# Turning the short row blocks of an attention with all 128 rows, and shifting one head's keys in the copies out of PSUM

## The chip, the core and the metric

The kernel runs on one core of one Trainium2 chip. A core has five engines with a queue each: TensorE (PE; its weight loads are listed apart as PEld), VectorE (DVE), ScalarE (ACT), GpSimd (POOL) and SyncE (SP), which here issues nearly all transfers between HBM and SBUF. TensorE writes to PSUM; the other engines read from there. The metric is the device time of one execution in microseconds (us), as a median of several runs.

## The reference

Three layers follow each other, for a batch of 4, all in float32:

```python
def _attn_ref(q, k, v):                  # 4 x 8 heads x 576 rows x 64
    ...                                  # q and k are rotated by position
    scores = scale * np.matmul(q_rot, k_rot.transpose(0, 1, 3, 2))
    scores = scores - np.max(scores, axis=-1, keepdims=True)
    attn = np.exp(scores)
    attn = attn / (np.sum(attn, axis=-1, keepdims=True) + 1e-09)
    return np.matmul(attn, v)

def _moe_ref(x, mu_k, mu_r, w_k, w_v, w_r):   # x: 4 x 576 x 512
    ...                                  # xk, xr: mixes of a row and the row before
    k = np.maximum(xk @ w_k, 0.0)
    v = k * k @ w_v
    return 1.0 / (1.0 + np.exp(-(xr @ w_r))) * v

def _moe2_ref(x, w_in, w_spatial, b_spatial, w_out):
    h = np.maximum(x @ w_in, 0.0)
    ...                                  # u, v: halves of h; v is normalized, mixed over rows
    return (u * v_s) @ w_out
```

## The kernel before

**Units.** The attention works on pairs of heads: 16 pairs, four in a batch entry, with the two heads of a pair on partitions 0 to 63 and 64 to 127. The 576 rows of a pair are four blocks of 128 rows and a rest of 64. A *unit* is one block of 128 rows for both heads of a pair. The rests of two neighbouring pairs make one unit together, the *tail*: its tile of exponentials has, for each pair u, the 64 rows of the first head on partitions 0 to 63 and those of the second on 64 to 127. `which` gives nine units for two pairs, the fifth of them the tail; there are 72 units and eight tails.

**A unit's steps.** `scores` (TensorE, into the two-buffered PSUM tile `s`), `top` (VectorE: the two maxima, line 342), `expo` (ScalarE: the two exponentials with their sums into `pf`, called p or P, line 347), `total`, `norm` and `spread` (sum, reciprocal, and the reciprocals laid out as `rb`, lines 351, 354, 358), three `turn` steps (TensorE) and three `take` steps (two on ScalarE, one on VectorE), and for each two units one `values` (TensorE, line 402) and `gather` (VectorE, line 414). `turn` transposes P, since the multiplication with V needs the keys on the partitions: it multiplies a block of P, as the loaded weights, with an identity matrix, and the result stands in a PSUM tile `t`, of which there are two in turn. `take` copies it to the SBUF tile `pt`.

**The layout of `pt`.** Ten chunks of up to 320 columns. Chunks 0 to 3 hold the first head's keys 0 to 511, chunks 4 to 7 the second head's keys 64 to 575, chunk 8 the first head's keys from 512 (partitions 0 to 63) and the second head's keys 0 to 63 (partitions 64 to 127), and chunk 9 the reciprocals. So the second head's chunks begin 64 keys on. Columns 256 to 319 belong to the tail.

**A tail's turns before.** `turn(0)` and `turn(1)` (line 367) take one head n each, for both pairs: eight transposes of 64 rows by 128 keys, beginning at key 64 n. Both need both exponentials (line 431). `turn(2)` (line 373) puts the last or first 64 keys and the reciprocals into place by eight multiplications of 64 x 64, which are 16 instructions on the chip. `take` copies once for each pair: 128 x 256 for n = 0, 1 (ScalarE), 128 x 128 for n = 2 (VectorE), line 395. For other units the turns are lines 378, 380 and 381.

**What sets the order.** All steps of the attention and of the second layer's feed-forward part are given to `Plan` (`add`, `order`, from line 57 on) with an engine, an assumed cost, the steps that must be done before, and a rank. `order` simulates the five engines with these costs and always starts next, on the engine that is free first, the step with the lowest rank among those that could start soon; the sequence that comes out is the program's order on each engine. So another cost or another dependency of one step can move other steps too. A batch entry's feed-forward multiplications (`mk`, line 498, and `mv`, line 537, on TensorE) have ranks that spread them over the units of the next batch entry. The first batch entry's 18 units have none beside them.

Functions that the change touches, and what calls them:

## Time and profile before

| | |
|---|---|
| median of 3 runs | 777.41 us (776.02 to 779.28) |
| the profiled execution's own time | 777.82 us |
| its span, first to last instruction | 776.0 us |
| busy: TensorE, VectorE, ScalarE | 740.8, 481.0, 463.6 us |
| transposes of a tail (line 367) start at | 33.3, 78.2, 129.4, 189.1, 246.3, 303.8, 361.2, 416.8 us |
| last transposes of all (line 378) | 444 us |
| feed-forward multiplications begin | 108.9 us |

The span is what the trace covers; the rest of the execution's own time lies around it. Busy times of one engine can't be added to those of another, since the engines run beside each other. What follows 446 us is the gate and the third layer, in which TensorE multiplies with little pause. In rows of the timeline a matmul's duration overlaps with that of the next one; what TensorE takes for a group is read from the starts of one group to the next.

### The profile page before, as it was taken

To read this page: it belongs to the slowest core of one execution; us is meant where nothing else is said; L and a number is where in the kernel's file an instruction comes from. 1 tells how busy PE (TensorE), PEld (TensorE's weight loads), DVE (VectorE), ACT (ScalarE), POOL (GpSimd) and SP (SyncE) were. 2 spreads that over 40 slices of the span, in tenths; PEclk is the share of its full clock that TensorE was granted. 3 is DMA by queue.
4 is the path that set the end of the run, shared out by engine and by line. 5 is a ranking of instruction groups with operands and counts; after the bars stand their busy time and mean duration, and the time that the engine had idled before them with its cause. 6 is when DMAs were issued, how large, how long until landed. Compare 5 with 4: busy or idle time off the path is not lost.

```text
span 776.0 us, 14283 instructions
## 1 busy us (share of the span) xinstructions
PE 740.8 (95%) x5696; PEld 649.9 (84%) x5696; DVE 481.0 (62%) x881; ACT 463.6 (60%) x1061; POOL 112.2 (14%) x132
## 2 busy tenths in 40 slices
PE   4788889999999999999999999999999999999997
PEld 2555569788888888888888898989989999998997
DVE  5988898888777877687856434246463342545111
ACT  3878898778777878778777644245333322533221
POOL 1432424011211211211111000002020000101000
PEclk9999999999999999999999999999999999999999
DMA  8363540542342442533232175072201212010101
GB/s 294 116 201 122 175 129 20 164 149 99 134 163 85 141 156 88 182 113 126 92 131 70 51 268 210 24 264 57 87 1 62 63 46 77 17 31 1 62 1 62
DMA packets 35268, 84.13 MB, mean 108 GB/s; under 512 B 4545, under 2 KB 10433, under 8 KB 35202
## 3 DMA queue, kind: packets, MB, share of 16 engines
q1 hardware_dynamic: 34658, 82.63, 31.6%
q8 instruction: 45, 0.74, 0.4%
q10 hardware_dynamic: 544, 0.59, 0.3%
q14 instruction: 21, 0.17, 0.1%
HBM read 60.65 MB, written 22.55 MB: 107 GB/s over the span
## 4 chain that ended last, share of the span: by engine, by line
PE 88%; DVE 4%; ACT 3%; DMA 3%; issue 0%; SPq 0%; ACTq 0%
PE mv L537 13%; PE mk L498 11%; PE v L402 11%; PE t L378 9%; PE sp L673 8%; PE r L673 7%; PE u L673 7%; PE hv L737 6%; PE o L673 6%; PE s L330 6%; PE s L338 3%; ACT pf L347 1%; DVE raw L249 1%; DMA wi<-wd 1%; PE s L327 1%; DVE sm L342 1%
## 5 line engine op out<-in xcount | busy, mean ns | idle before, releaser
L342 DVE TENSOR_REDUCE sm<-s 128x1 f32<-128x576 f32 x144 | 107.2, 751 | 36.9 <-PE s L330 30.5
L347 ACT ACTIVATE pf<-s,sm 128x576 f32<-128x576 f32 x144 | 107.0, 745 | 14.1 <-DVE sm L342 13.0
L537 PE MATMUL mv<-kh,wv 128*128 128x288 f32 x512 | 114.1, 305 | 1.2 <-ACT kh L512 1.2
L498 PE MATMUL mk<-x,wk 128*128 128x288 f32 x768 | 110.2, 298 | 0.4 <-ACT rl L505 0.4
L395 ACT COPY pt<-t 128x512 f32<-128x512 f32 (+1 forms) x160 | 84.8, 542 | 34.3 <-PE t L378 32.0
L498 PEld LDWEIGHTS mk<-x,wk 128*128 128x128 f32 x768 | 102.9, 188 | 0.7 <-ACT rl L505 0.6
L378 PE MATMUL t<-ident,pf 128*128 128x128 f32 x512 | 82.5, 284 | 14.0 <-ACT pf L347 14.0
L537 PEld LDWEIGHTS mv<-kh,wv 128*128 128x128 f32 x512 | 85.6, 191 | 5.4 <-issue 3.9
L378 PEld LDWEIGHTS t<-ident,pf 128*128 128x128 f32 x512 | 56.6, 141 | 39.9 <-issue 16.4
L402 PE MATMUL v<-pt,vt 128*64 128x256 f32 (+1 forms) x640 | 87.5, 411 | 0.0
L537 PE MATMUL mv<-kl,wv 128*128 128x288 f32 x256 | 76.5, 299 | 0.6 <-DVE kl L516 0.6
L402 PEld LDWEIGHTS v<-pt,vt 128*64 128x64 f32 x640 | 44.3, 136 | 31.7 <-issue 4.1
L673 PE MATMUL sp<-ws,vn 128*128 128x288 f32 x384 | 53.9, 295 | 0.0
L673 PE MATMUL r<-xr,wr 128*128 128x288 f32 x384 | 52.5, 296 | 1.2 <-ACT vs L543 1.2
L673 PE MATMUL o<-g,wo 128*128 128x288 f32 x384 | 52.9, 296 | 0.5 <-ACT os L796 0.5
L673 PEld LDWEIGHTS r<-xr,wr 128*128 128x128 f32 x384 | 51.7, 188 | 1.8 <-ACT vs L543 1.5
L673 PEld LDWEIGHTS sp<-ws,vn 128*128 128x128 f32 x384 | 52.4, 188 | 0.7
L673 PEld LDWEIGHTS o<-g,wo 128*128 128x128 f32 x384 | 51.7, 188 | 1.4 <-ACT os L796 1.2
L673 PE MATMUL u<-x,wi 128*128 128x288 f32 x384 | 52.0, 296 | 0.0
L673 PEld LDWEIGHTS u<-x,wi 128*128 128x128 f32 x384 | 51.6, 188 | 0.3
L537 PEld LDWEIGHTS mv<-kl,wv 128*128 128x128 f32 x256 | 48.9, 191 | 1.2 <-DVE kl L516 1.2
L249 DVE TENSOR_TENSOR raw<-raw,cst 128x1152 f32<-128x1152 f32 (+1 forms) x34 | 45.6, 1344 | 5.7 <-DMA raw<-kp 4.9
(347 smaller groups left out, 1200.3 us busy)
## 6 DMA issues: line engine op xcount, KB each, us to landing
raw<-kp SPq DMA_DIRECT2D x15, 576.0 KB, 3.8
raw<-qp SPq DMA_DIRECT2D x15, 576.0 KB, 4.3
vt<-vp SPq DMA_DIRECT2D x16, 320.0 KB, 3.8
xd<-xt SPq DMA_DIRECT2D x16, 288.5 KB, 3.2
vd<-vs SPq DMA_DIRECT2D x32, 144.0 KB, 1.8
v<-vd SPq DMA_DIRECT2D x16, 288.0 KB, 2.7
out<-os SPq DMA_DIRECT2D x15, 288.0 KB, 2.1
wi<-wd SPq DMA_DIRECT2D x8, 512.0 KB, 9.1
```

The source lines that it names most:

```text
L249: nc.vector.tensor_tensor(t["raw", k][:, :, z], t["raw", k][:, :, z], cst[:, :, z], op=ALU.mult)
L330: nc.tensor.matmul(ps[j][:, h, :HALF], t[a, 0][r, 128 * c:128 * c + 128], t[b, 1][r, x], **f)
L338: nc.tensor.matmul(o, q[r, 128 * c:min(128 * c + 128, S)], k[r, h * HALF:(h + 1) * HALF], start=True, stop=True)
L342: nc.vector.tensor_reduce(st["sm"][:, 0, j:j + 1], st["s"][j][:, :, :HALF], axis=AX.XY, op=ALU.max, negate=True)
L347: nc.scalar.activation(st["p"][:, j, :].rearrange("p (a b) -> p a b", a=2), st["s"][j][:, :, :HALF], AF.Exp, bias=st["sm"][:, 0, j:j + 1], ...
L378: nc.tensor.transpose(pt[:, c, :], p[:, n, k:k + 128], ident)
L395: nc.scalar.copy(o, x) if eng == "ACT" else nc.vector.tensor_copy(o, x)
L402: nc.tensor.matmul(pv[HEAD[j], z], v[:, 4 * j + c if c < 4 else 8 + j, :], pt[:, 4 * j + c if c < 4 else 8, z], start=c == 0, stop=c == 4)
L498: nc.tensor.matmul(ps[:, :HALF], wk[w][:, c, fc * 128:(fc + 1) * 128], a[:, c, :], start=k == 0, stop=k == 11)
L537: nc.tensor.matmul(xs["v", dc][:, :HALF], wv[w][:, fc, dc * 128:(dc + 1) * 128], a, start=k == 0, stop=k == 23)
L673: nc.tensor.matmul(ps[:, h, :HALF], w, a[:, h * HALF:(h + 1) * HALF], start=m == 0, stop=m == n - 1)
L737: nc.tensor.matmul(ps[:, :FS], x[a][:, d, c:c + 128], wi[w][:, d, FS:], start=k == 0, stop=k == 11)
```

## The change

A tail's `turn(0)` and `turn(1)` now take one pair each instead of one head: four transposes of all 128 rows (both heads' rests) by 128 keys, beginning at key 0 for both heads. Each needs only its own pair's exponentials. `turn(2)` transposes the 64 keys from 512 on, with all 128 rows, once for each pair, and turns the reciprocals with four multiplications of 64 x 64 as before. By source calls a tail has 14 turns in place of 24. Since the second head's chunks begin 64 keys on, the copies put its halves from one half of the partitions to the other: `take` has three copies for n = 0, 1 (128 x 256 and two of 64 x 256) and six for n = 2 (four of 64 x 64, two of 128 x 64). The layout of `pt` changes so that these halves lie in a row: chunk 8 becomes chunk 4, and the second head's chunks become 4 (upper half) to 8. The costs that the plan assumes for the tail's turns and copies change with it, and a `take` of n = 0, 1 now belongs to one pair's `pt` alone.

```diff
         def turn(n, slot):
...
-            if tail and n < 2:
+            if tail and n == 2:
                 for u in range(2):
-                    for c in range(4):
-                        k = 64 * n + 128 * c
-                        nc.tensor.transpose(pt.rearrange("p c (h q) -> p (c h) q", h=2)[:, 4 * u + c, :],
-                                            p[HEAD[n], u, k:k + 128], ident[HEAD[n], HEAD[n]])
-            elif tail:
+                    nc.tensor.transpose(pt[0:64, u, :], p[:, u, 512:], ident)
                 for u in range(2):
-                    for k in range(2):
-                        for j, r in enumerate(HEAD):
-                            nc.tensor.matmul(pt[r, u, HEAD[k]], st["r"][r, u, :] if k else p[r, u, 512 - 512 * j:576 - 512 * j],
-                                             ident[r, r], start=True, stop=True)
+                    for j, r in enumerate(HEAD):
+                        nc.tensor.matmul(pt[r, 2 + u, 0:64], st["r"][r, u, :], ident[r, r], start=True, stop=True)
             elif n < 2:
                 for c in range(4):
-                    k = 64 * n + 128 * c
+                    k = (0 if tail else 64 * n) + 128 * c
                     nc.tensor.transpose(pt[:, c, :], p[:, n, k:k + 128], ident)
...
         def take(n, eng):
...
+            if not tail:
+                o = into[0]["pt"][:, :, 128 * part:128 * part + 128]
+                copy(o[:, 5 * n:5 * n + 4, :] if n < 2 else o[:, 4:10:5, :], x if n < 2 else x[:, 0:2, :])
+            elif n < 2:
+                o = into[n]["pt"]
+                copy(o[:, 0:4, z], x[:, :, lower])
+                copy(o[upper, 4:8, z], x[lower, :, upper])
+                copy(o[lower, 5:9, z], x[upper, :, upper])
+            else:
+                for u, d in enumerate(into):
+                    copy(d["pt"][lower, 4, z], x[lower, u, lower])
+                    copy(d["pt"][upper, 8, z], x[lower, u, upper])
+                    copy(d["pt"][:, 9, z], x[:, 2 + u, 0:64])
...
-        ready = [[exps[m, 0], exps[m, 1]] if tail else [exps[m, 0]], [exps[m, 1]], [sp]]
+        ready = [exps[m, 0], exps[m, 1], sp]
...
-            turned[m, n] = add("PE", (0.5, 0.5, 0.8)[n] if tail else (0.44, 0.44, 0.22)[n], lambda slot, n=n: turn(n, slot),
-                               ready[n], m + 0.1 * n, take="t", kind="t")
+            turned[m, n] = add("PE", (0.44, 0.44, 0.75 if tail else 0.22)[n], lambda slot, n=n: turn(n, slot),
+                               [ready[n]], m + 0.1 * n, take="t", kind="t")
...
-            x = add(eng, ((0.68, 0.68, 0.55) if tail else (0.59, 0.59, 0.42))[n], lambda n=n, eng=eng: take(n, eng),
-                    [turned[m, n]] + [y for d in into for y in freed.get(d["n"] - PTB, [])], m - 0.2, give=turned[m, n])
+            to = into if n == 2 else into[n if tail else 0:][:1]
+            x = add(eng, (1.13, 1.13, 0.95)[n] if tail else (0.59, 0.59, 0.42)[n], lambda n=n, eng=eng: take(n, eng),
+                    [turned[m, n]] + [y for d in to for y in freed.get(d["n"] - PTB, [])], m - 0.2, give=turned[m, n])
```

The order moves with it. TensorE at the first tail, before: s_379 are scores of unit 5, t_1 and t_2 the tail's turns 1 and 2, t_0_421 the first turn of unit 5, v_426 the multiplication with V of the first pair's tail, s_453 and s_454 the scores of unit 6.

```order
L338 MATMUL s_379<-rot_1_259,rot_0_262 128x288
L367 MATMUL t_1_389<-ident,pf_357 128x64 x8
L373 MATMUL t_2_405<-ident,pf_357 64x64 x2
L373 MATMUL t_2_405<-ident,rb_401 64x64 x2
...
L378 MATMUL t_0_421<-ident,pf_415 128x128 x4
L402 MATMUL v_426<-pt_290,vt_134 64x320 x10
L338 MATMUL s_453<-rot_1_259,rot_0_262 128x288
L338 MATMUL s_454<-rot_1_259,rot_0_262 128x288
```

The same place in the change; the line numbers are the changed kernel's, v_441 is the multiplication with V, s_427 and s_428 are the scores of unit 6, s_479 those of unit 7, t_0_495 unit 6's first turn.

```order
L338 MATMUL s_373<-rot_1_259,rot_0_262 128x288
L372 MATMUL t_1_384<-ident,pf_357 128x128 x4
L365 MATMUL t_2_402<-ident,pf_357 64x128 x2
L368 MATMUL t_2_402<-ident,rb_397 64x64 x4
L372 MATMUL t_0_416<-ident,pf_399 128x128 x4
L338 MATMUL s_427<-rot_1_259,rot_0_262 128x288
L338 MATMUL s_428<-rot_1_259,rot_0_262 128x288
...
L402 MATMUL v_441<-pt_290,vt_134 64x320 x10
...
L338 MATMUL s_479<-rot_1_259,rot_0_262 128x288
...
L372 MATMUL t_0_495<-ident,pf_458 128x128 x4
```

The scores of unit 6 moved from behind the multiplication with V to ahead of it, and the first turn of unit 6 from ahead of unit 7's scores to behind them.

VectorE behind the second tail, before: pt_862 are the tail's copy and (last but one row) that of unit 14's reciprocals, x_0_0 a low half for the feed-forward part, xt_753 the gather, s_933 the scores of unit 15.

```order
L395 COPY pt_862<-t_2_875 128x2x64
L268 TENSOR_TENSOR rl_0_900<-raw_0_642,rh_0_842 128x576
L272 TENSOR_TENSOR qe_92<-raw_0_642,qe_91 64x64 x2
L354 RECIPROCAL sm_852<-sm_852 128x2
L156 TENSOR_SCALAR I-920_921<-I-686_687 128x512
L164 TENSOR_SCALAR I-686_687<-I-686_687 128x512
L165 SCALAR_TENSOR_TENSOR I-920_921<-I-920_921,I-686_687 128x512
L479 TENSOR_TENSOR x_0_0_926<-mt_0_0_464,x_0_0_925 128x288
L414 TENSOR_TENSOR xt_753<-v_904,pt_766 128x320
L342 TENSOR_REDUCE sm_935<-s_933 128x1
L395 COPY pt_862<-t_2_954 128x2x128
L342 TENSOR_REDUCE sm_935<-s_934 128x1
```

The same place in the change, from the second maximum of unit 14 on; s_924 and s_926 belong to unit 15.

```order
L342 TENSOR_REDUCE sm_836<-s_835 128x1
L156 TENSOR_SCALAR I-897_898<-I-682_683 128x512
L268 TENSOR_TENSOR rl_0_901<-raw_0_638,rh_0_882 128x576
...
L354 RECIPROCAL sm_836<-sm_836 128x2
L480 TENSOR_TENSOR x_0_0_907<-mt_0_0_490,x_0_0_906 128x288
L414 TENSOR_TENSOR xt_749<-v_886,pt_762 128x320
L480 TENSOR_TENSOR x_0_0_907<-mt_0_1_664,x_0_0_906 128x288
L164 TENSOR_SCALAR I-682_683<-I-682_683 128x512
L165 SCALAR_TENSOR_TENSOR I-897_898<-I-897_898,I-682_683 128x512
L385 COPY pt_864<-t_2_944 128x2x128
L342 TENSOR_REDUCE sm_926<-s_924 128x1
```

A second low half of x and the copy of unit 14's reciprocals moved from behind unit 15's first maximum to ahead of it.

## Rows read from the trace of the kernel before

**Rows 1.** Stretches, us: their length, then each engine's busy time (instructions); clock, DMA.
```profile
20.00:40.00 20.00, 15.50 (x128) 10.00 (x128) 19.08 (x35) 16.51 (x43) 7.95 (x7) 1.00 0.35 118
80.00:100.00 20.00, 16.60 (x129) 10.18 (x125) 17.70 (x36) 17.29 (x45) 8.52 (x7) 1.00 0.53 167
340.00:380.00 40.00, 40.00 (x351) 34.41 (x349) 33.57 (x63) 33.39 (x87) 5.82 (x7) 1.00 0.31 108
```

**Rows 2.** Timeline, TensorE, a late tail: start us, us, engine, line, operation, names, form, count.
```profile
189.05 0.59 PE L367 MATMUL t<-ident,pf 64*128 64x64 f32 x6
...
189.42 0.40 PE L330 MATMUL s<-rh,rh 64*128 64x288 f32 x1
...
190.38 0.60 PE L367 MATMUL t<-ident,pf 64*128 64x64 f32 x7
...
190.90 0.33 PE L373 MATMUL t<-ident,pf 64*64 64x64 f32 x4
...
191.52 2.91 PE L402 MATMUL v<-pt,vt 128*64 128x320 f32 x20
```

**Rows 3.** Timeline, TensorE, an ordinary unit.
```profile
176.02 0.66 PE L378 MATMUL t<-ident,pf 128*128 128x128 f32 x4
...
176.60 0.54 PE L330 MATMUL s<-rh,rh 64*128 64x288 f32 x4
...
176.98 0.44 PE L330 MATMUL s<-rl,rh 64*128 64x288 f32 x4
...
177.24 0.44 PE L330 MATMUL s<-rh,rl 64*128 64x288 f32 x4
...
177.61 0.66 PE L378 MATMUL t<-ident,pf 128*128 128x128 f32 x4
...
178.21 0.27 PE L381 MATMUL t<-ident,rb 128*128 128x128 f32 x1
```

**Rows 4.** Timeline, weight loads, two places; in brackets the idle time before.
```profile
41.21 0.79 PEld L338 LDWEIGHTS s<-rot,rot 64*128 64x128 f32 x8 [0.49 <-issue]
...
176.60 0.30 PEld L330 LDWEIGHTS s<-rh,rh 64*128 64x128 f32 x4 [0.17 <-issue]
```

**Rows 5.** Timeline, ScalarE, the first tail.
```profile
36.35 0.64 ACT L395 COPY pt<-t 128x256 f32<-128x256 f32 x2
...
38.23 0.22 ACT L347 ACTIVATION_READ_ACCUMULATOR pf<-s,sm 128x1 f32 x1
```

**Rows 6.** Groups by form, VectorE: count, busy us, mean ns, idle before.
```profile
L395 DVE COPY pt<-t 128x256 f32<-128x256 f32 x64 | 27.1, 423 | 9.1 <-PE t L381 7.0
...
L479 DVE TENSOR_TENSOR x<-mt,x 128x288 fp32r<-128x288 f32 x32 | 14.7, 481 | 4.0 <-ACT x L476 3.9
...
L395 DVE COPY pt<-t 128x128 f32<-128x128 f32 x16 | 3.8, 281 | 0.0
```

**Rows 7.** Waits of TensorE, 0:140 and 120:446: us in total, times, longest.
```profile
PE t L378 <- ACT pf L347: 14.0, 12, 1.8
...
PE t L380 <- ACT pt L395: 0.5, 1, 0.5
```

**Rows 8.** Timeline, TensorE, first tail to unit 8.
```profile
38.37 2.91 PE L402 MATMUL v<-pt,vt 128*64 128x320 f32 x20
...
41.21 1.24 PE L338 MATMUL s<-rot,rot 64*128 64x288 f32 x8
...
45.04 1.50 PE L338 MATMUL s<-rot,rot 64*128 64x288 f32 x8
...
51.22 1.24 PE L338 MATMUL s<-rot,rot 64*128 64x288 f32 x8
```

**Rows 9.** Timeline, VectorE, the first and the second tail.
```profile
36.04 1.40 DVE L342 TENSOR_REDUCE sm<-s 128x1 f32<-128x576 f32 x2
...
39.03 1.33 DVE L249 TENSOR_TENSOR raw<-raw,cst 128x1152 f32<-128x1152 f32 x1
...
87.39 0.76 DVE L342 TENSOR_REDUCE sm<-s 128x1 f32<-128x576 f32 x1 [0.66 <-PE s L338]
```

More of the change, by code (lines that the diff above doesn't have):

```diff
@@ L383, in take @@
         def take(n, eng):
-            for u, d in enumerate(into):
+            for d in into if n == 2 else into[n if tail else 0:][:1]:
                 if "pt" not in d:
                     d["pt"] = at.tile([128, 10, 320], F32, tag=f"pt{d['n'] % PTB}", name=f"pt{d['n']}")
-                o = d["pt"][:, 4 * n:min(4 * n + 4, 10), 256:320]
-                if not tail:
-                    o, x = d["pt"][:, 4 * n:min(4 * n + 4, 10), 128 * part:128 * part + 128], st["t", n]
-                    x = x if n < 2 else x[:, 0:2, :]
-                elif n < 2:
-                    x = st["t", n].rearrange("p c (h q) -> p (c h) q", h=2)[:, 4 * u:4 * u + 4, :]
-                else:
-                    x = st["t", n][:, u, :].rearrange("p (h q) -> p h q", h=2)
-                nc.scalar.copy(o, x) if eng == "ACT" else nc.vector.tensor_copy(o, x)
+            copy = nc.scalar.copy if eng == "ACT" else nc.vector.tensor_copy
+            x, z, (lower, upper) = st["t", n], slice(256, 320), HEAD
+            if not tail:
[11 more added lines that the diff above has]
+                    copy(d["pt"][:, 9, z], x[:, 2 + u, 0:64])
         def values(slot):
@@ L402, in values @@
                     nc.tensor.matmul(pv[HEAD[j], z], v[:, 4 * j + c if c < 4 else 8 + j, :],
-                                     pt[:, 4 * j + c if c < 4 else 8, z], start=c == 0, stop=c == 4)
+                                     pt[:, 5 * j + c if c < 4 else 4, z], start=c == 0, stop=c == 4)
         def rows(i):
@@ L430, in unit @@
         sp = add("ACT", 0.26, spread, [nm], m - 0.3)
-        ready = [[exps[m, 0], exps[m, 1]] if tail else [exps[m, 0]], [exps[m, 1]], [sp]]
+        ready = [exps[m, 0], exps[m, 1], sp]
         for n in range(3):
-            turned[m, n] = add("PE", (0.5, 0.5, 0.8)[n] if tail else (0.44, 0.44, 0.22)[n], lambda slot, n=n: turn(n, slot),
-                               ready[n], m + 0.1 * n, take="t", kind="t")
+            turned[m, n] = add("PE", (0.44, 0.44, 0.75 if tail else 0.22)[n], lambda slot, n=n: turn(n, slot),
+                               [ready[n]], m + 0.1 * n, take="t", kind="t")
             eng = ("ACT", "ACT", "DVE")[n]
-            x = add(eng, ((0.68, 0.68, 0.55) if tail else (0.59, 0.59, 0.42))[n], lambda n=n, eng=eng: take(n, eng),
-                    [turned[m, n]] + [y for d in into for y in freed.get(d["n"] - PTB, [])], m - 0.2, give=turned[m, n])
-            for d in into:
+            to = into if n == 2 else into[n if tail else 0:][:1]
+            x = add(eng, (1.13, 1.13, 0.95)[n] if tail else (0.59, 0.59, 0.42)[n], lambda n=n, eng=eng: take(n, eng),
+                    [turned[m, n]] + [y for d in to for y in freed.get(d["n"] - PTB, [])], m - 0.2, give=turned[m, n])
+            for d in to:
                 d["ev"].append(x)
```

## The prediction

> **What bounds the kernel now.** I read the stretches of the span first, then the order of work at the tails, then single tails in the timeline. In the table by stretches the reader is to compare TensorE with the other engines: TensorE is busy 40.00 of 40.00 us in the middle of the joint stage, against 33.57 on VectorE and 33.39 on ScalarE, but 15.50 and 16.60 of 20 us in two stretches ahead of 100 us, where VectorE has 19.08 and 17.70 [rows 1]. So there are two regimes. From about 120 us to the end of the attention, where six of the eight tails lie, the multiplications of the feed-forward part fill every gap, and only TensorE's own time counts. Ahead of that, with two tails, each unit's scores, maxima, exponentials and next scores make a chain through three engines, and what stands in a queue ahead of a link counts. The rest of the program has no tail and I leave it alone.
>
> **The tails that TensorE bounds.** A tail before: from the first narrow transpose at 189.05 to the multiplication with V at 191.52 are 2.47 us [rows 2]. That holds 16 transposes of 64 rows (six in the 0.37 us from 189.05 to 189.42, so 0.062 us each), twelve score multiplications of the next unit, which run in the same array shape and are woven in, and 16 small instructions in 0.62 us from 190.90 to 191.52, so 0.039 us each with the way out. One change of array shape stands ahead of it and is not in the 2.47.
>
> Its parts after, from an ordinary unit [rows 3]: five full transposes start in the 0.60 us from 177.61 to 178.21, so 0.12 us each; four score multiplications in the 0.26 us from 176.98 to 177.24, so twelve in 0.80. A change of shape: 176.02 to 176.60 is 0.58, less four transposes (0.48), leaves 0.10; 177.24 to 177.61 is 0.37, less 0.26, leaves 0.11. The weight loads pause 0.17 us at such a place, and 0.49 us where the long multiplications with V go before [rows 4]. I take 0.12 us and keep 0.10 and 0.49 as ends.
>
> - Eight full transposes: 8 x 0.12 = 0.96. Scores: 0.80.
> - Two transposes of a 128 x 64 block. The trace has none; from below the 64-row transposes' 0.062, from above the full ones' 0.12. They stream as many identity columns as the full ones, so I take 0.12: 0.24.
> - Four multiplications of the reciprocals, eight instructions as now at 0.039: 0.31.
> - Changes of shape: full to 64 rows for the scores, and back, since the tail's second transposes are now full; into the 128 x 64 shape; from it to 64 x 64. Four times 0.12: 0.48. (The way out is in the 0.039.)
>
> The sum is 2.79, against 2.47 + 0.12 = 2.59: 0.2 us more per tail. Fewer instructions save 0.16, but three more changes of shape are to be paid as I count them (the way from 64 x 128 to 64 x 64 was inside the 2.47). Six tails: +1.2 us. With 0.10 per change and the cheaper blocks it is +0.02 per tail, hence 0; with 0.17 it is 0.35, hence +2.1.
>
> The Trainium skill speaks for the old form here: its page TensorEngine Tiling (Array Packing), section Theoretical Speedup, gives a contraction of at most 64 a factor of up to two. By that the sixteen would cost half of 0.99 us and the change would lose another 0.5 us per tail, 3 us in six; but the trace has them at 0.062 us one after another, in one half of the rows at a time, so the sum goes by the row.
>
> **The copies.** A tail's two ScalarE steps go from two copies of 128 x 256 to three of as many columns, two of them on 64 partitions; a pair takes 0.64 us [rows 5], so I take 0.32 each, bounded by half of that if half the partitions cost half, and by 0.64 if the shift costs as much again. That adds 0.64 us per tail (0.32 to 1.28). VectorE goes from two copies of 128 columns (281 ns) to six of 64. From 256 to 128 columns the mean falls from 423 to 281 ns [rows 6], 1.1 ns a column, so 64 columns cost about 0.21 us alone; bounds 0.10 (half of 128's) and 0.28 each, and 0.175 taken in a row of six. Six are 1.05 us against 0.48: +0.57 per tail (0.1 to 1.2). In the six late tails TensorE's feed-forward work hides both: from 120 us to the attention's end it waited once for such a copy, 0.5 us, and for nothing else [rows 7]. If that cover went, each tail could lose about that 0.5. In the early tails I count them below. The other units' copies and the multiplications with V keep shape and number; their blocks lie in other places of the same tile, which I take at nothing, since a column's distance appears in no term here.
>
> **The first tail (33 to 51 us).** The changed order puts the scores of unit 6 ahead of the tail's multiplication with V on TensorE. Before, V runs 38.37 to 41.28 and the scores start at 41.21 [rows 8], though the exponential they wait for has its sum read out by 38.45 [rows 5]. After, ScalarE reaches that point 0.3 us later (one copy of the second step), so the scores start near 38.8. VectorE is then the late one: its two maxima end at 37.44, and rotary work holds it until 40.36 [rows 9]; with 0.57 more of copies until 40.93. Two maxima (1.40) bring it to 42.3. From 37.44 to 38.45 the second exponential followed in 1.0, so unit 7's scores start near 43.4, not 45.04. From there to unit 8's scores were 6.18 us (45.04 to 51.22); unit 6's first four transposes move into that piece (+0.48), giving 50.1 for 51.22. I take -1.1 us. Ends: -2.4 if the whole move lasts; +1.2 if nothing of it lasts and both engines' extra copies are on the path.
>
> **The second tail (78 to 96 us).** Here V goes ahead of the next unit's first transposes, which had waited for an exponential; such a wait is 1.2 us in the mean (14.0 in 12, [rows 7]), and unit 15's scores can start sooner by as much. But on VectorE the order now has two more steps ahead of that unit's first maximum: the second low half of x (481 ns, [rows 6]) and the copy of reciprocals and last keys (423 ns). With the 0.57 of small copies that is 1.47 us, and before, VectorE had 0.66 us to spare there [rows 9]. So the maximum comes 0.8 us later. I take +0.8 at this place; as the two steps are only moved, some is given back: ends -1.2 and +1.4. DMA issues change places too by a few rows in the stretch of the late tails; TensorE waited for no load there [rows 7], so I take nothing.
>
> **The sum.** +1.2 - 1.1 + 0.8 = +0.9 us on the profiled execution's 777.82 us (span 776.0 and 1.8 around it), so 778.7. That execution lies 0.4 us over the median of 777.41, so I forecast 778.3 us. A measurement of this kernel tells about 0.5% from no change, 3.9 us here; so the forecast is no change.
>
> **Rivals.**
> 1. *Slower: the changes of shape cost more than 0.12 us.* Place: between a late tail's last transposes, the 128 x 64 blocks, the reciprocals and the scores. At a price s, a tail goes from 2.47 + s to 2.31 + 4s: 3s - 0.16. The early tails give -0.3, so +3.9 in all needs 0.70 per tail, or s = 0.29: from there on it decides. At 0.49, 1.31 per tail, six give +7.9 and the time is 785.0. For it: the 0.49 pause. Against: that pause follows 20 long multiplications, and the starts of TensorE's own rows moved by 0.10 and 0.11 only. The same page of the Trainium skill says, in section Key Properties, that changing the tiling mode drains the engine. By that rule each change would cost the end of the transpose before it, 0.27 us in the row at 178.21, so 0.65 per tail and 781.0 us; the rows show less than half of it. Chance of a price from 0.29 up: 0.13.
> 2. *Faster: the early start lasts.* If VectorE makes up the moved steps in unit 16, the second tail gives -1.2, the first -2.4; if the pauses hide under the transposes that run, a late tail saves 0.16, six 1.0. That is -4.6 and 772.8. For it: the transposes fall from 24 to 14 per tail by source calls, and the first needs one exponential for two. Against: VectorE is over 88% busy in both early stretches. Chance 0.09.
> 3. *The copies take the place.* The second transposes' buffer comes free only after three copies; if each late tail waited 0.5 us, as in the one wait of [rows 7], +3.0 and 781.3. For it: ScalarE at 83% in a late stretch. Against: 12 feed-forward multiplications are put between a late tail's pieces in the new order at most of the tails. Chance 0.12.
>
> That the change does nothing of what it says is out: the new order has the full transposes and the new copies at every tail. It remains 0.66 for the forecast, whose own range from the bounds of its terms is 776 to 781.
>
> **How the numbers follow.** The low end, 774, takes the first tail's -2.4 and the second's -1.2 with no loss late (777.4 - 3.6 = 773.8). The high end, 782.5, takes +2.1 late and +1.4 and +1.2 early (782.1), and reaches into rivals 1 and 3. Faster than 773.5 asks for all of rival 2: 0.08. Slower than 781.3 is rival 1, half of rival 3 and 0.01 of the rest: 0.13 + 0.06 + 0.01, together 0.20. Within: 0.72.
>
> **What would show it.** In the changed kernel's timeline: a late tail's steps on TensorE, set apart from feed-forward work, at 2.8 us; pauses of 0.10 to 0.17 at four places; unit 6's scores near 38.8 and unit 8's near 50.1; unit 15's first maximum later against its scores than before; TensorE at 40.00 of 40 in the late stretches, with no wait for a copy. Wrong would be: waits of TensorE for the tail's copies, pauses near 0.3 or 0.5 in the tails, or a start of the full stretch that lies more than 2 us off the old one.

## The result, and the profile after

The changed kernel takes 783.82 us (median of 7 runs, 781.31 to 786.44) against 777.53 us (776.02 to 779.79) for the kernel before on the same chip: a ratio of 1.0071, 95% interval 1.0054 to 1.0087. It is slower, by more than the 0.5% that a measurement tells; the forecast was 778.3, within 774 to 782.5. The profiled spans are 782.6 and 776.0 us. Part of the difference is TensorE's clock: at a granted clock of 0.997 the changed kernel took 781.31 and 781.76 us, and the kernel before, in the executions beside the experiments, on five chips, 777.56 to 779.08; so some 3 us remain at the same clock.

To see where 6.6 us went, I compared the two traces by work done: all of TensorE's multiplications other than transposes and the tails' small ones are the same in both, so for each moment of the trace before I asked when the changed kernel had begun as much of that work. That difference is called the lag below; it is worked out from the start times in the timeline, from one execution of each kernel, so a stretch at half clock that only one of them has is in it. It is -0.2 us at 100, -2.4 at 120, -1.3 at 135, +3.6 at 165, +5.8 at 446 and +6.6 at the end. So the changed kernel leads when the full stretch begins, loses 5 us behind the third tail, 2 us in the five tails after it, and 0.8 after the attention.

Stretches of the changed kernel, columns as in [rows 1]:

```profile
80.00:100.00 20.00, 16.08 (x113) 9.79 (x113) 17.33 (x38) 17.40 (x45) 7.71 (x7) 1.00 0.53 165
135.00:140.00 5.00, 2.62 (x24) 1.88 (x22) 4.97 (x10) 3.56 (x9) 3.04 (x2) 0.95 0.71 204
140.00:145.00 5.00, 4.95 (x25) 4.35 (x26) 2.96 (x6) 3.61 (x9) 2.33 (x2) 0.50 0.08 30
340.00:380.00 40.00, 40.00 (x335) 34.98 (x334) 30.56 (x63) 31.40 (x80) 7.00 (x7) 1.00 0.39 133
```

The first and the last look like those before. The second does not: TensorE works for 2.62 of 5 us while VectorE works for 4.97, and in the third the granted clock is 0.50, that is 1.2 GHz. The timeline of TensorE shows the hole, behind the third tail:

```profile
135.18 0.65 PE L372 MATMUL t<-ident,pf 128*128 128x128 f32 x4
...
137.35 0.27 PE L375 MATMUL t<-ident,rb 128*128 128x128 f32 x1
140.05 1.11 PE L372 MATMUL t<-ident,pf 128*128 128x128 f32 x4 [2.42 <-ACT pf L347]
141.09 1.04 PE L330 MATMUL s<-rh,rh 64*128 64x288 f32 x4
...
144.21 0.59 PE L538 MATMUL mv<-kh,wv 128*128 128x288 f32 x1
```

The same place in the kernel before, one unit behind the third tail:

```profile
138.11 0.66 PE L378 MATMUL t<-ident,pf 128*128 128x128 f32 x4
139.25 0.33 PE L380 MATMUL t<-ident,pf 128*128 128x128 f32 x1 [0.48 <-ACT pt L395]
...
139.44 0.38 PE L537 MATMUL mv<-kh,wv 128*128 128x288 f32 x1
```

Before, feed-forward work (`mv`) follows at once and TensorE never stops for more than 0.48 us. After, two units stand one behind the other with nothing between them: all `mk` has been issued, and the first `mv` starts at 144.21 in place of 139.44. TensorE waits 2.42 us for unit 24's exponential, and then four transposes take 1.11 us instead of 0.65. What the exponential waits for stands on VectorE, whose timeline there is:

```profile
135.71 1.02 DVE L164 TENSOR_SCALAR I-1402_1403<-I-1402_1403 128x512 int32<-128x512 int32 x1
136.76 0.69 DVE L165 SCALAR_TENSOR_TENSOR I-1551_1552<-I-1551_1552,I-1402_1403 128x512 int32<-128x512 int32 x1
137.37 0.75 DVE L509 TENSOR_TENSOR rl<-rl 128x576 f32<-128x576 f32 x1
138.04 0.42 DVE L385 COPY pt<-t 128x256 f32<-128x256 f32 x1
138.38 1.42 DVE L342 TENSOR_REDUCE sm<-s 128x1 f32<-128x576 f32 x2
139.70 0.75 DVE L517 TENSOR_TENSOR kl<-rl,kh 128x576 fp32r<-128x576 f32 x1
```

The scores were finished about 136.8, and their maxima start at 138.38, behind the work on weights and the feed-forward part, without a gap. The last row is the fourth `kl`; the plan starts no `mv` before all four and the weights for it. It comes later than before, and so do the last of these weights (ScalarE has its part of them done at 140.50 us, before at 133.90), though `mk` began 2 us sooner. The same `kl` before:

```profile
138.20 0.74 DVE L516 TENSOR_TENSOR kl<-rl,kh 128x576 fp32r<-128x576 f32 x1
```

The waits of TensorE from 120 to 446 us, answering to the second row of [rows 7]:

```profile
PE t L372 <- ACT pf L347: 4.0, 3, 2.4
```

The copies cost somewhat more than the prediction took, by form (count, busy us, mean ns); these answer to [rows 5, 6], and the last row is ScalarE's copies of the tails before:

```profile
L390 ACT COPY pt<-t 64x256 f32<-64x256 f32 x16 | 5.9, 370 | 0.2
L389 ACT COPY pt<-t 64x256 f32<-64x256 f32 x16 | 5.8, 365 | 0.2
L388 ACT COPY pt<-t 128x256 f32<-128x256 f32 x16 | 5.8, 364 | 2.5 <-PE t L372 2.2
...
L395 DVE COPY pt<-t 128x64 f32<-128x64 f32 x16 | 3.6, 225 | 0.4
L394 DVE COPY pt<-t 64x64 f32<-64x64 f32 x16 | 3.5, 218 | 0.2
L393 DVE COPY pt<-t 64x64 f32<-64x64 f32 x16 | 3.3, 209 | 0.8 <-PE t L368 0.8
...
L395 ACT COPY pt<-t 128x256 f32<-128x256 f32 x32 | 10.3, 379 | 1.0 <-PE t L367 0.9
```

The first tail answers to [rows 8]; the scores of units 6, 7 and 8 start at 39.12, 44.06 and 50.48 (38.8, 43.4 and 50.1 were predicted):

```profile
39.12 1.37 PE L338 MATMUL s<-rot,rot 64*128 64x288 f32 x8
...
44.06 1.24 PE L338 MATMUL s<-rot,rot 64*128 64x288 f32 x8
...
50.48 1.24 PE L338 MATMUL s<-rot,rot 64*128 64x288 f32 x8
```

### The profile page after: what moved, and what is told of

The parts are those of the page before. It is cut to its first block, busy times and chain, and to the rows that moved or that the text cites. A ratio compares the mean times of both kernels' runs of the same rounds, so it can differ in the third digit from the quotient of the medians.

```text
span 782.6 us, 14086 instructions
## 1 busy us (share of the span) xinstructions
PE 744.6 (95%) x5584; PEld 651.9 (83%) x5584; DVE 485.1 (62%) x913; ACT 470.2 (60%) x1077; POOL 111.1 (14%) x132
## 4 chain that ended last, share of the span: by engine, by line
PE 88%; ACT 4%; DVE 3%; DMA 3%; issue 1%; SPq 0%; ACTq 0%; DVEq 0%
PE mv L538 13%; PE mk L499 11%; PE v L402 10%; PE t L372 9%; PE sp L674 8%; PE r L674 7%; PE u L674 7%; PE hv L738 6%; PE o L674 6%; PE s L330 6%; PE s L338 3%; ACT pf L347 2%; PE s L327 1%; DMA wi<-wd 1%; DMA wr<-wd 1%; PE t L374 1%
## 5 line engine op out<-in xcount | busy, mean ns | idle before, releaser
L499 PE MATMUL mk<-x,wk 128*128 128x288 f32 x768 | 113.2, 300 | 1.1 <-ACT rl L506 1.1
L372 PE MATMUL t<-ident,pf 128*128 128x128 f32 x576 | 93.6, 286 | 18.7 <-ACT pf L347 18.7
L372 PEld LDWEIGHTS t<-ident,pf 128*128 128x128 f32 x576 | 64.3, 142 | 47.5 <-ACT pf L347 20.1
L385 ACT COPY pt<-t 128x512 f32<-128x512 f32 x128 | 74.7, 584 | 38.9 <-PE t L372 38.2
```

What stands on the lines that cost most here:

```text
L372: nc.tensor.transpose(pt[:, c, :], p[:, n, k:k + 128], ident)
L385: copy(o[:, 5 * n:5 * n + 4, :] if n < 2 else o[:, 4:10:5, :], x if n < 2 else x[:, 0:2, :])
L499: nc.tensor.matmul(ps[:, :HALF], wk[w][:, c, fc * 128:(fc + 1) * 128], a[:, c, :], start=k == 0, stop=k == 11)
```

## The experiments

The experiments ran on five chips. Each ratio is to the kernel before on the same chip, so across chips the ratios compare, not the times. Only ScalarE and VectorE copy out of PSUM in these kernels.

### Order and copies apart

Is it the order, or the work? This kernel keeps the changed `turn`, `take` and V layout, with the plan's costs and dependencies of before, so that the order is that of before outside the tails:

```diff
-        ready = [exps[m, 0], exps[m, 1], sp]
+        ready = [[exps[m, 0], exps[m, 1]] if tail else [exps[m, 0]], [exps[m, 1]], [sp]]
...
-            x = add(eng, (1.13, 1.13, 0.95)[n] if tail else (0.59, 0.59, 0.42)[n], lambda n=n, eng=eng: take(n, eng),
+            x = add(eng, ((0.68, 0.68, 0.55) if tail else (0.59, 0.59, 0.42))[n], lambda n=n, eng=eng: take(n, eng),
```

> The changed turns and copies, but in the order of before: the plan's costs and dependencies for the tails are those of before. Theory A (the order: behind the third tail the new sequence leaves TensorE without feed-forward work while VectorE is late, 2.4 us of waiting, and the clock then falls to half for 6.8 us, 3.4 us lost): 778.7 us, that is before + 1.2 for the tails' own time on TensorE (a late tail 2.8 us for 2.6), no wait over 1 us between 110 and 446 us, and one stretch at half clock only, near 470 us as before. Theory B (the work itself: the extra copies hold up the exponentials and so TensorE): 781 to 784 us, with waits behind late tails in this order too.

Measured: 785.49 us (783.59 to 786.78), ratio 1.0083 (1.0061 to 1.0105). The loss is there without any change of order. The lag is +0.9 at 60 us, +3.6 at 90, +3.9 at 135 and +7.8 at 446.

The opposite, old turns and copies with the new plan. Here V of a tail can stand ahead of a copy it should follow, since the new plan counts a copy for one pair alone, so that part of P is not the right one:

```diff
-            if tail and n == 2:
+            if tail and n < 2:
...
-            for d in into if n == 2 else into[n if tail else 0:][:1]:
+            for u, d in enumerate(into):
```

> The turns, copies and layout of before, in the changed kernel's order. Theory A: 781 to 783 us, with a wait of 1.5 us or more behind the third tail (VectorE and ScalarE have 0.6 us less to do per tail) and, mostly, the clock at half behind it. Theory B: 777 to 778 us, no such wait.

Measured: 785.5 us (783.77 to 786.53), ratio 1.0081 (1.006 to 1.0102), with a wait of 2.7 us behind the third tail. Against the kernel before, order alone costs as much as work alone.

Then the changed turns with as few copies as before, in either order. The shift by 64 keys is left out, so part of P is not the right one:

```diff
-                copy(o[upper, 4:8, z], x[lower, :, upper])
-                copy(o[lower, 5:9, z], x[upper, :, upper])
+                copy(o[:, 4:8, z], x[:, :, upper])
...
-                    copy(d["pt"][lower, 4, z], x[lower, u, lower])
-                    copy(d["pt"][upper, 8, z], x[lower, u, upper])
-                    copy(d["pt"][:, 9, z], x[:, 2 + u, 0:64])
+                    copy(d["pt"][:, 8:10, z], x[:, 2:4, 0:64])
```

> The changed turns on TensorE in the order of before, but with as many copies out of PSUM as before: two per ScalarE step of a tail, and two on VectorE in place of six. The shift by 64 is left out, so the keys of each pair's second head land in wrong places of P. If the extra copies cost the time: within 0.3% of before (777.5 to 780.5), the drift at the late tails +0.2 each and no new waits behind them. If TensorE's new turns cost it, by their instructions or what they do to the clock: as the whole change in the old order, 784 to 787 (ratio 1.006 to 1.010).

> The changed kernel in its own order with as many copies as before (two per ScalarE step, two on VectorE); the shift by 64 is left out. It completes the square of order and copies: old order with few copies 778.4, with many 785.5; new order with many 783.8. If the new order costs by itself through the third tail: 781 to 784. If the copies are the whole loss: 775 to 778, below before by the head's 2 us.

The changed turns' square, each with its ratio to the kernel before:

| | copies as before | the change's copies |
|---|---|---|
| order of before | 778.4 us, 0.9988 (0.9971 to 1.0005) | 785.49 us, 1.0083 (1.0061 to 1.0105) |
| order of the change | 783.39 us, 1.0061 (1.0039 to 1.0083) | 783.82 us, 1.0071 (1.0054 to 1.0087) |

So the new turns on TensorE show no cost and no gain; with the added copies the old order costs 6.4 us against the kernel before; the new order costs 4.8 us with no added copy; and the two don't add up. In the new order the lead at 120 us is 3.6 us with few copies and 2.4 with many, but both lose about 5 us behind the third tail. With few copies TensorE's rows there read:

```profile
136.18 0.27 PE L375 MATMUL t<-ident,rb 128*128 128x128 f32 x1
139.22 1.12 PE L372 MATMUL t<-ident,pf 128*128 128x128 f32 x4 [2.77 <-ACT pf L347]
```

The upper left kernel also gives the tail's own price on TensorE, the term of 2.79 us:

```profile
188.95 0.60 PE L372 MATMUL t<-ident,pf 128*128 128x128 f32 x4
189.48 0.53 PE L330 MATMUL s<-rh,rh 64*128 64x288 f32 x4
...
190.12 0.43 PE L330 MATMUL s<-rh,rl 64*128 64x288 f32 x4
190.47 0.66 PE L372 MATMUL t<-ident,pf 128*128 128x128 f32 x4
190.97 0.38 PE L365 MATMUL t<-ident,pf 128*64 128x128 f32 x2
191.28 0.45 PE L368 MATMUL t<-ident,rb 64*64 64x64 f32 x8
191.66 0.76 PE L399 MATMUL v<-pt,vt 128*64 128x320 f32 x4
```

It is 2.71 us, from 188.95 to 191.66. The lag of this kernel grows by 0.4 us in all from 120 to 446 us, where the prediction had 1.2.

### Which engine's copies

The kernel before with copies that only repeat what was just written, on ScalarE (two per tail) or VectorE (four per tail):

```diff
+                if tail and n < 2 and u:
+                    nc.scalar.copy(o[HEAD[0]], x[HEAD[0]])
```

> The kernel before with one more copy of 64 partitions x 256 in each of a tail's two ScalarE steps (it writes again what the copy before it wrote); TensorE and VectorE do what they did. 16 copies of about 0.365 us are 5.8 us of ScalarE. If ScalarE's added copies cost most of the time: 781 to 785 (ratio 1.005 to 1.009), with waits of 0.5 to 0.9 us behind the late tails on the exponentials. If VectorE's do, or the two only together: 777 to 780.

```diff
+                if tail and n == 2:
+                    for r in HEAD:
+                        nc.vector.tensor_copy(o[r, 0], x[r, 0])
```

> The kernel before with four more copies of 64x64 in each tail's VectorE step (again what was just written). 32 copies of about 0.215 us are 6.9 us of VectorE. If ScalarE's added copies are what costs: 777 to 780 here. If VectorE's are, by putting off the maxima that stand behind them: 781 to 785.

ScalarE: 780.08 us, ratio 1.0015 (0.9994 to 1.0036), not told from no change; its lag grows by 0.9 us from 120 to 446, and by 2.5 at the second tail, where this execution has a stretch at half clock from 80.5 us. VectorE: 784.1 us, ratio 1.0052 (1.0027 to 1.0078), and from 120 to 446 by 5.3. VectorE there, behind the fifth tail (start, us):

```profile
249.67 1.42 DVE L342 TENSOR_REDUCE sm<-s 128x1 f32<-128x576 f32 x2 [0.30 <-PE s L330]
251.01 0.28 DVE L395 COPY pt<-t 128x128 f32<-128x128 f32 x1
251.32 0.46 DVE L398 COPY pt<-t 64x64 f32<-64x64 f32 x2
251.81 0.29 DVE L395 COPY pt<-t 128x128 f32<-128x128 f32 x1
252.14 0.46 DVE L398 COPY pt<-t 64x64 f32<-64x64 f32 x2
...
257.05 0.76 DVE L342 TENSOR_REDUCE sm<-s 128x1 f32<-128x576 f32 x1
```

The same in the kernel before:

```profile
247.95 1.42 DVE L342 TENSOR_REDUCE sm<-s 128x1 f32<-128x576 f32 x2 [0.30 <-PE s L330]
249.29 0.48 DVE L395 COPY pt<-t 128x128 f32<-128x128 f32 x2
...
253.98 0.76 DVE L342 TENSOR_REDUCE sm<-s 128x1 f32<-128x576 f32 x1
```

From the first maxima to the next unit's it is 7.38 us against 6.03, in both without a gap: VectorE is full there, though its share of the span is 62%. In the kernel before it works for 8.5 to 9.9 of 10 us behind each of the six late tails. The copies push the next maximum, and with it the exponential and the transposes that wait for it.

Then the change's copies by number and length, one engine's at a time (in the old order, the other engine's as in the kernels with few copies). The shift is left out again, and ScalarE's copies here are all on 128 partitions, which by the rows above take as long as those on 64:

> The changed turns in the old order with ScalarE's three copies per step (12 over both pairs' chunks, lengths as in the change) but VectorE's last step at two copies as before; the shift by 64 of the ends is left out. If VectorE's copies are the larger part: 778.5 to 781 (ratio 1.000 to 1.004). If ScalarE's are: 782 to 785.

> The counterpart: the changed turns in the old order, ScalarE at two copies per step as before, VectorE at six small copies; the shift of the second head's keys is left out. If VectorE's copies are the larger part: 782 to 785.5 (ratio 1.005 to 1.009). If ScalarE's: 778 to 781.

ScalarE's alone: 781.38 us, 1.0038 (1.0021 to 1.0055). VectorE's alone: 780.97 us, 1.0024 (1.0004 to 1.0043). My expectation that VectorE's are the larger part failed for the whole time: 3.1 and 2.7 us, not told apart. By the lag from 120 to 446 us they are 1.3 and 2.9, each with the 0.4 us of the turns in it, while ScalarE's lose another 1.3 ahead of 90 us. Together they cost 4.2 in this stretch, which is the sum, and 6.4 in all for a sum of 5.8, within the intervals.

### Full VectorE, or place?

The same four copies, from the scores' bank to a tile that nothing reads, ahead of or behind the second maximum of the unit behind a tail; the second has these lines behind the reduction, with `["s"][1]`:

```diff
         def top(j):
+            if m % 9 == 5 and j == 1:
+                junk = at.tile([128, 2, 64], F32, tag="junk", bufs=1, name=f"junk{m}")
+                for r in HEAD:
+                    for u in range(2):
+                        nc.vector.tensor_copy(junk[r, u, :], st["s"][0][r, u, 0:64])
             nc.vector.tensor_reduce(...)
```

> The kernel before with four copies of 64x64 from the scores' PSUM bank to a scratch tile that nothing reads, put on VectorE between the first and the second maximum of the unit behind each tail; tails, copies of P and TensorE as before. If what costs is that the second maximum stands behind 0.9 us of copies: as the four extra copies into P (784.1), 782 to 785, 0.5 to 1.3 us at each late tail. If it was V or the release of the turns' PSUM tile that waited for the copies into P: 777 to 780.

> The same four copies into the scratch tile put right behind the second maximum: the same VectorE work per unit, one place later. If the place ahead of the maximum is what costs: 777 to 780 (ratio 0.999 to 1.003). If it is VectorE's work as such (its share of 62% made longer by 6.9 us): 782 to 785, as with the copies ahead.

Ahead: 784.48 us, 1.0071 (1.0045 to 1.0097). Behind: 780.99 us, 1.0024 (1.0005 to 1.0044). By the totals the place decides; by the lag it does not where I meant it to. In the six late tails the two lose 3.3 and 2.7 us from 120 to 446 us; the difference is at the second tail, where the first has +3.2 by 90 us, with a stretch at half clock in it, and the second +0.2. So in the late tails these copies cost nearly as much behind the maximum as ahead of it, though P and TensorE's work are as before.

If VectorE's time is what counts there, taking other work off it must give the loss back. The rest of this product is left out, so the results are not the right ones:

```diff
+                y = z if i < 2 else slice(0, 128)
-                nc.vector.tensor_tensor(t["raw", k][:, :, z], t["raw", k][:, :, z], cst[:, :, z], op=ALU.mult)
+                nc.vector.tensor_tensor(t["raw", k][:, :, y], t["raw", k][:, :, y], cst[:, :, y], op=ALU.mult)
```

> The changed turns and copies in the old order (785.5, ratio 1.008), with VectorE relieved of other work where it stands busy without a gap behind the tails: the multiplication by cosine and sine (128x1152, 1.34 us) covers 128 of 576 columns from the third head pair on, about 1 us less beside each late tail; the rest of that multiplication is left out. If the copies cost because VectorE is full there (9.81 of 10 us at 190 to 200 us in the kernel before): the late tails' loss goes, 777 to 781. If ScalarE's copies or the tile's release cost: 783 to 786.

> The control: the kernel before with the same multiplication cut short. TensorE is busy for all of 180 to 446 us there, so VectorE's relief should give little: 775.5 to 778.5, no more than 0.3% below before. If it gave 4 us or more, the relief in the kernel with the changed turns would say nothing of the copies.

With the change's work: 783.47 us, 1.0068 (1.0046 to 1.009), where it was 1.0083. Before: 776.51 us, 0.998 (0.9965 to 0.9995). In the total this failed: by the ratios the relief gives 1.2 us to the one and 1.6 to the other, not told apart. In the stretch from 120 to 446 us it holds in part. TensorE's idle time there, 326 us less its busy time in the table by stretches:

| kernel (old order) | TensorE busy | idle |
|---|---|---|
| before | 325.52 | 0.48 |
| changed turns, copies as before | 325.65 | 0.35 |
| with ScalarE's copies | 325.33 | 0.67 |
| with VectorE's copies | 324.50 | 1.50 |
| with both | 323.33 | 2.67 |
| with both, short rotary product | 325.09 | 0.91 |
| before, short rotary product | 326.00 | 0.00 |

The row of the kernel with both, and that with the short product, in which VectorE (third) falls from 252.97 to 235.67:

```profile
120.00:446.00 326.00, 323.33 (x2673) 274.67 (x2672) 252.97 (x483) 255.86 (x640) 56.46 (x51) 1.00 0.35 116
```

```profile
120.00:446.00 326.00, 325.09 (x2696) 276.50 (x2693) 235.67 (x484) 256.02 (x642) 53.66 (x51) 1.00 0.35 117
```

1.76 of 2.19 us of added idle time go; but the same relief takes the 0.48 us of the kernel before too, so 1.28 of the 2.19 go beyond what it does there. TensorE's waits tell which. From 120 to 446 us with both engines' copies, then the same with the short product:

```profile
PE t L374 <- ACT pt L385: 1.6, 2, 1.4
PE t L372 <- ACT pf L347: 0.8, 3, 0.5
```

```profile
PE t L375 <- ACT pt L386: 0.7, 2, 0.4
```

The waits for exponentials are gone; those for ScalarE's copies of ordinary units' P stay in part. By the lag the stretch costs 1.8 us with the relief for 4.2 without, while the kernel before gains 1.1 from it; so with VectorE relieved in both, 2.9 of the 4.2 us are still lost. VectorE's queue is shown as a part of the late tails' loss, then, and not as all of it. What the copies cost at the second tail is not given back: the lag at 90 us is 4.0 with the relief and 3.6 without, both with a stretch at half clock from 85 us.

### The hole behind the third tail

First, work to fill it, in the changed kernel: 20 transposes of the unit matrix behind unit 23's last turns.

```diff
+                if m == 23:
+                    for d in range(20):
+                        nc.tensor.transpose(pt[:, 2 + d % 2, :], ident, ident)
```

> The changed kernel with 20 transposes of the identity, which nobody reads, behind the last turns of unit 23, where TensorE had nothing for 2.4 us behind the third tail. Theory A says that the pause is what brings the clock down there: 780.4 us (3.4 less than the changed kernel), no half clock between 130 and 150 us; the waiting itself stays, since the exponentials come no sooner. Theory C (the clock falls for another reason, or anyhow): no less than 783 us and the half clock stays.

Measured: 786.06 us, 1.0097 (1.0073 to 1.0121). As built it tells nothing: VectorE's copy of that tile waited 1.72 us for the added transposes, and the maxima behind it came later. The second try puts them into unit 24's own tile, ahead of its transposes:

```diff
+                for d in range(20 if m == 24 and n == 0 else 0):
+                    nc.tensor.transpose(pt[:, d % 4, :], ident, ident)
                 for c in range(4):
```

> The changed kernel with 20 transposes of the unit matrix (about 2.3 us) put on TensorE ahead of unit 24's first turns, where it stood still for 2.4 us; nothing waits for them but those turns. If that pause is what drops the clock: no stretch at half clock at 139 to 146 us, and 3 us less than the changed kernel, 779.5 to 781.5. If the clock falls whatever fills the pause, or the time is lost again further on: 783 to 785.

Measured: 784.09 us, 1.0057 (1.0035 to 1.0078), not told from the changed kernel's 1.0071. The stretch that was at half clock is at full clock, but in this execution another one, of 5 us in the head, is not:

```profile
55.00:60.00 5.00, 5.00 (x27) 3.63 (x27) 3.04 (x6) 2.30 (x6) 0.00 (x0) 0.66 0.38 118
...
140.00:145.00 5.00, 4.96 (x45) 4.42 (x44) 4.37 (x8) 4.50 (x12) 2.95 (x3) 1.00 0.26 101
```

From 135 to 165 us it loses 2.6 us where the changed kernel lost 4.9. So by these two executions about half of the loss behind the third tail is the pause and half the clock; for the total the expectation failed.

Last, feed-forward work held back in the plan, so that some `mk` stands in the hole:

```diff
-        first = 18 * (b + 1) + 9 * h + 2.0
+        first = 18 * (b + 1) + 9 * h + 2.0 + (1.6 if b == h == 0 else 0)
```

> The changed kernel with the first feed-forward group's rank 1.6 units later in the plan, so that 12 of its multiplications stand between the two units behind the third tail, where the changed kernel has none and waited 2.4 us. If that wait, with the half clock behind it, is what the new order lost: 779 to 781.5 (3 us less than the changed kernel's 783.8). If VectorE, busy for 4.97 of 5 us there, only moves the wait on to the next unit: 783 to 786.

Measured: 785.69 us, 1.0082 (1.0059 to 1.0105). The rival expectation holds: there is no wait of 2.4 us, but waits of 1.1, 1.1, 0.8 and 0.8 us in its place, and the granted clock is 0.74 from 130 to 135 us, ahead of the old place.

### Three ways to make the copies cheaper

Full turns for all three steps, with the first pair's second head or the second pair's first head shifted, and four copies of 64x2x64 on VectorE instead of six, in the old order:

```diff
-            if tail and n == 2:
...
-                    k = (0 if tail else 64 * n) + 128 * c
+                    k = 64 * n + 128 * c
...
+            elif n == 1:
+                o = into[1]["pt"]
+                copy(o[:, 5:9, z], x[:, :, upper])
+                copy(o[upper, 0:4, z], x[lower, :, lower])
+                copy(o[lower, 1:5, z], x[upper, :, lower])
```

> The order of before; turns 0 and 1 of a tail as in the change, but the second pair begins at key 64, so that its first head is the one that is shifted, and turn 2 is two full transposes as in an ordinary unit (the 64 keys 512 on of the first pair beside the keys 0 to 63 of the second; the reciprocals), with four copies of 64 x 128 in place of six small ones. Three changes of the array's shape and eight small multiplications fall away per tail. Theory A with the prices of the prediction: a late tail takes 0.96 + 0.80 + 0.24 + 2 x 0.12 = 2.24 us for 2.59, so 6 x -0.35 = -2.1: 775.4 us. Theory B: 780 us or more.

Measured: 786.57 us, 1.0098 (1.0075 to 1.0121). TensorE has fewer turns in a tail, but it waits 3.5 us in all, at four places from 120 to 450 us, for ScalarE's copies of turned P.

Four of VectorE's six copies on ScalarE, in the old and in the new order:

```diff
-                    copy(d["pt"][lower, 4, z], x[lower, u, lower])
-                    copy(d["pt"][upper, 8, z], x[lower, u, upper])
+                    nc.scalar.copy(d["pt"][lower, 4, z], x[lower, u, lower])
+                    nc.scalar.copy(d["pt"][upper, 8, z], x[lower, u, upper])
```

> The changed turns and copies in the old order (ratio 1.008 before), with the four copies of 64x64 of each tail's last step on ScalarE, so that VectorE has two copies per tail as before and ScalarE ten in place of four. If VectorE's copies cost the time, because the second maximum of the next unit stands behind them: the late tails lose 0.1 to 0.3 us each and the time is 778 to 781 (ratio 1.000 to 1.003). If any copy between a tail and V costs its own length on whichever engine: 784 to 787 again, since ScalarE takes on 0.9 us per tail.

> The same move of four copies to ScalarE in the changed kernel's own order (the plan counts 0.55 us for VectorE's two). The head is then 2 us earlier at the start of the feed-forward work, and the wait behind the third tail (2.4 us in the changed kernel) should be about 0.9 us shorter. If the copies on VectorE are the cause: 777 to 780. If the new order itself costs (the feed-forward work of the third tail used up): the clock falls again at 139 us and 781 to 784.

Measured: 793.99 us, 1.0189 (1.0162 to 1.0217), and 788.34 us, 1.0112 (1.0087 to 1.0137). Both expectations missed by far. VectorE's rows behind the fourth tail in the old order:

```profile
197.45 0.75 DVE L342 TENSOR_REDUCE sm<-s 128x1 f32<-128x576 f32 x1
199.65 0.23 DVE L395 COPY pt<-t 128x64 f32<-128x64 f32 x1 [1.45 <-ACT pt L394]
200.36 0.22 DVE L395 COPY pt<-t 128x64 f32<-128x64 f32 x1 [0.48 <-ACT pt L394]
200.51 0.75 DVE L342 TENSOR_REDUCE sm<-s 128x1 f32<-128x576 f32 x1
```

The copies into one tile wait for each other, so VectorE stands still for 1.93 us with a maximum behind it, and ScalarE's last two copies wait in turn, with two exponentials behind them. A step split over two queues made both wait. None of the kernels that leave nothing out came in under the kernel before.

## Why the prediction was wrong

**The step that failed** is the one on which the rest stood: "From about 120 us to the end of the attention ... the multiplications of the feed-forward part fill every gap, and only TensorE's own time counts", and with it "In the six late tails TensorE's feed-forward work hides both". The full stretch was read from the trace of before as a property of the place. It was a property of an order: before, 36 `mv` stand behind the first unit after the third tail. The new order uses up `mk` sooner, and the last `kl` for `mv` is ready later (140.46 us for 138.94), so the lead ends in a pause of 2.42 us with a stretch at 1.2 GHz behind it; 5 us go there. And in the old order, where the cover is the same, the copies still cost: 4.2 us of lag from 120 to 446 us, for which the forecast had nothing but TensorE's 1.2. Part of that is shown to be VectorE's queue, in which they stand ahead of the next unit's maxima; the rest is not shown. TensorE in 40.00 of 40 us did not tell how much cover was left: that stretch, which the prediction named as a sign, reads 40.00 in both kernels. From 120 to 446 us TensorE had 0.48 us of idle time, and the added copies, 0.9 us per tail on ScalarE and 0.8 on VectorE, brought it to 2.67.

**TensorE's own term** (+0.2 per tail) came out as +0.12 in the tail shown, 2.71 for 2.59; by the lag of that one execution the net loss was 0.4 us in six, not 1.2, and the total shows none (0.9988, 0.9971 to 1.0005). The changes of shape were over-priced: in the tail above, four transposes of 0.12 from 188.95 leave 0.05 to the scores, four scores in 0.26 from 190.12 leave 0.09, four transposes from 190.47 leave 0.02, and two blocks, taken at 0.12 each, from 190.97 leave 0.07, all below the 0.12 that I took. The first rival, a price from 0.29 up, is out.

**The copies** were taken too cheap, at 0.32 us for the 0.365 of ScalarE's and 0.175 for the 0.21 to 0.225 of VectorE's, with half the partitions as dear as all. By the rows of busy time a tail has 0.90 us more on ScalarE where 0.64 was taken, and 0.82 on VectorE for 0.57, both within the bounds given. The larger fault was their place in the sum.

**The early tails.** First tail: -0.7 us at unit 8's scores (50.48 for 51.22), -1.1 forecast; the second tail took back 0.2 by the lag (-0.3 at 74 us, -0.2 at 90), +0.8 forecast. Its mechanism was the forecast one: unit 15's scores start 1.6 us sooner (84.53 us for 86.11), but its first maximum comes at 87.65 for 87.39, behind the steps that moved ahead of it. The faster rival was half right: the full stretch did begin 2 us earlier (106.88 for 108.92), but the lead did not last.

**The third rival**, each late tail waiting 0.5 us for a copy, came nearest: 781.3. That is luck as far as its wait goes: the waits in the old order are those shown above, 1.6 us for copies of ordinary units' P and 0.8 for exponentials, and none for the tails' own copies. All the idle time that TensorE has more than before, 2.19 us, is about half of the 4.2 us that the six tails lose.

**Left open:** why order and copies together cost hardly more than either alone; what the part of the late tails' loss is that neither TensorE's idle time nor VectorE's relief accounts for; and why the second tail costs 2.3 to 2.7 us of lag in the executions in the old order that have a stretch at half clock from 80 to 85 us there, and 0 to 0.7 in those with no such stretch in the head. The clock is not what the old order with both engines' copies loses: its one execution at a granted clock of 1.000 took 783.59 us, and the kernel before at 0.999 took 775.95 to 776.96.

## What to carry to other kernels

An engine that is busy all the time in a stretch is not a cover of any size: look in its order for how much independent work is still queued behind the place you change, and whether a faster start uses it up before the next batch is ready. Look at the other engines in stretches of 5 or 10 us behind the place, not at their shares of the span: here VectorE, at 62% of the span, was full for 7.38 us where copies were added. And copies that move work from a matmul engine to the copying engines must be priced per instruction, since half the partitions did not make them shorter.

## What the runs showed of the hardware

- A copy out of PSUM on 64 partitions took about as long as one on 128: 365 and 370 ns against 364 on ScalarE (256 columns), 209 and 218 against 225 on VectorE (64 columns).
- After a pause of 2.42 us that followed a busy stretch, the granted clock of TensorE was 0.50 from 140 to 145 us; the same forms took 1.11 us for four transposes and 1.04 for four scores there, against 0.65 and 0.53 at full clock. With the pause filled by transposes of the unit matrix it was 1.00. The pause of 2.77 us in the new order with few copies was followed by 0.50 from 140 to 145 us too. A pause of 2.73 us in the changed kernel, behind the second tail, was not: the granted clock stayed at 1.00 from 80 to 100 us.

```profile
89.31 0.66 PE L372 MATMUL t<-ident,pf 128*128 128x128 f32 x4 [2.73 <-ACT pf L347]
```

- Changing the shape of the array between a tail's groups cost an estimated 0.02 to 0.09 us of TensorE's time, what the starts from 188.95 to 191.28 us leave at 0.12 us for a transpose or block and 0.26 for four scores.
